# Softmax row sums of twenty attention heads taken by fours instead of by pairs, and late loads moved

## The chip, the cores and the metric

The kernel runs on one core of a Trainium2 chip. A core has a matrix engine (TensorE, PE in the profile; PEld is its weight load), a vector engine (VectorE, DVE), an activation engine (ScalarE, ACT), GpSimd (POOL) and a sync engine (SP), which run their own instruction streams in order and wait for each other by semaphores, and 16 DMA engines that move data between DRAM, SBUF and SBUF. SP and POOL issue most of the transfers; a transfer that adds to what lies at its destination (an accumulating DMA) is issued from POOL. The metric is the device time of one execution in microseconds, as the median of the runs.

## The reference, cut to what matters

```python
x = A_x                                             # 2048 rows of 1024
g = sigmoid((x * gate_w).sum(-1, keepdims=True))
# a: attention with 32 heads of 32
q, k, v = split(x @ wqkv)
p = softmax(einsum("bhqd,bhkd->bhqk", q, k) * 32 ** -0.5, axis=-1)
a = einsum("bhqk,bhkd->bhqd", p, v) -> (2048, 1024) @ wo
# b: for each row and each of 32 key heads the best of 8 x 8 experts, gelu(x . u[e]) * v[e]
return g * a + (1 - g) * b
```

All of it is float32. The change concerns the attention: the sum over keys in the softmax's denominator.

## The kernel before, in words

The program has three stages: projections and the expert branch (to about 648 us), the attention (to about 1650 us), and the output projection. The change lies in the attention; a few constants at the program's start and places in SBUF move with it.

**Tiles of the attention.** The 32 heads run one after another. A head has 16 tiles; tile `kt` holds 128 keys against all 2048 queries. `scores` makes four matmuls a tile (128 x 512 each) into a ring of seven PSUM banks (`ring`), ACT applies exp and writes the tile `P` (128 x 2048) to SBUF, and `pv` multiplies it with the values into the PSUM tile `o`. The loop at the end goes by groups of two tiles: scores of this group, then `pv` of the group before, then whatever the table `todo` holds for the two steps. A step is one tile, and `at(step, f, ...)` enters a function at a step; for head `h`, `base` is 16 h and `NT` is 16, so `base + NT + 12` is tile 12 of the head after `h`.

**Row sums.** A head's denominator is the sum of its 16 tiles over keys, that is over tiles and over the 128 partitions. Over tiles (`presum`): VectorE adds eleven times into `ACC`; tile 1 is written straight into a second sum `ACCD`, and tiles 3, 8 and 12 are added to `ACCD` by accumulating DMAs of 1 MB (`accd<-P` in the profile; where the buffer of a tile has another name, `accd<-vhl`, `accd<-wo_raw`). These three depend on each other, since each adds to what the one before left. In the next head ACC and ACCD are added on VectorE (merge). Over partitions: two heads share the tile `T` (named `rb` in the profile). An even head is merged into T and its lower 64 partitions are added onto the upper by an accumulating DMA (`merge_even`, `fold_even`); an odd head is merged in two halves by two VectorE instructions and its upper half is added onto T's lower (`merge_odd`, `fold_odd`). Then T holds one head in each half, and `head_sums(h, 2)` sums over 64 partitions each by four matmuls with the constant `ones2` (32 columns, 16 for each head). The four go as a set; ACT copies their bank out (`ssb`), SP stores it (`smd`), and after each fourth head `load_r` and `norm_r` load four heads' sums back, take the reciprocals and store them (`rr`, `rd`).

**Buffers of P.** `RING` says how many places the tiles of P rotate through: 11, from tile 330 on 9, from tile 384 on 8 (15 tiles a head count, since tile 1 is in ACCD). The three that go are the places of weights for the stage after the attention (`wo_raw2`, `wo_raw3`, `vhl`), loaded when they are free. A place is free when `pv` and the sum that reads it are done, for tiles 3, 8 and 12 when their DMA has landed.

**Order on the queues.** SP issues, for each head, the loads of K and Q of the head after the next (six of 256 KB and a small one; they wait for the last scores of the head that has their place), the store of `o` (`od<-osb`), a quarter of the next four heads' values (`V<-vd`), and in some heads a piece of a weight (`wo_raw<-in_wo`) and the sums' transfers. In the last heads come `vhl` and the attention's own outputs for the next stage (`V<-od`, 128 KB each). SP takes these strictly in order: a transfer that waits holds up all behind it. POOL issues the accumulating DMAs, in order as well.

Of the kernel before, what the change touches and what calls it, by code (L numbers as in the profile page):

```python
# [10 lines left out]
F32 = mybir.dt.float32  # L11
# [3 lines left out]
OP = mybir.AluOpType  # L15
# [4 lines left out]
H = 32  # L20
KC = D // 128
HC = KC // 2
NT = S // 128
NQ = S // 512
# [8 lines left out]
def gated_mha_peer_kernel(ctx, tc, xT, wqkv, wv, wo, wq, k12, ug, v, out):  # L33
# [8 lines left out]
    nc = tc.nc  # L42
# [25 lines left out]
    cbits = const.tile([1, 1], F32, name="cbits")  # L68

    ones2 = const.tile([128, 32], F32, name="ones2")  # L70
    nc.vector.memset(ones2, 0.0)
    for i in range(2):
        nc.vector.memset(ones2[64 * i:64 * i + 64, 16 * i:16 * i + 16], 1.0)


    const.tile([128, 24], F32, name="fill")
    ctx.enter_context(tc.tile_pool(name="fillr", bufs=1, side="right")).tile([128, 120], F32, name="fillr")

    def dma(dst, src, queue=nc.sync):
        a, b = (ap.bitcast(F32) if ap.dtype == F32R else ap for ap in (dst, src))  # L80
        return queue.dma_start(a, b)
# [621 lines left out]
    for blk, (k, n) in enumerate(order):  # L703
        w, c = chunks[k]
# [600 lines left out]
    def rowsum(ps, *srcs, ones=ones):  # L1305
        for src in srcs:
            for qc in range(NQ):
                yield nc.tensor.matmul(ps[32 * qc:32 * qc + 32, :], ones,  # L1308
                                       src[:, qc * 512:(qc + 1) * 512],
                                       start=(src is srcs[0]), stop=(src is srcs[-1]))  # L1310
# [15 lines left out]
    def merge(h):  # L1326
        nc.vector.tensor_add(ACC[h], ACC[h], ACCD[h])
# [13 lines left out]
    def fold_odd(h):  # L1341
        nc.gpsimd.dma_start(T[low], ACC.pop(h)[up], accum_op=OP.add)

    def head_sums(h, heads=1):
        i, = ring_banks(1)
        for ins in rowsum(ring[:, i, :], T if heads == 2 else ACC.pop(h),
                          ones=ones2 if heads == 2 else ones):
            on_ring(ins, i)
        on_ring(norm_sums(h, ring[:, i, :], heads), i)

# [7 lines left out]
    def norm_sums(h, ps, heads=1):  # L1358
        g, j = divmod(h, 4)
        o = wk.tile([128, 512], F32, name="ssb")  # L1360
        ins = nc.scalar.activation(o, ps, AF.Copy)
# [57 lines left out]
    def at(step, f, *a):  # L1419
        todo.setdefault(step, []).append((f, a))  # L1420

    for h in range(H):
        base = h * NT
        g, j = divmod(h, 4)
        if h >= 1 and h + 1 < H:
            at(base - 1, load_head, h + 1)
        if h < H - 1:
            at(base + NT, finish, h)
            if h == H - 2:
                at(base + NT + 5, merge, h)  # L1430
# [340 lines left out]
```

## Time and profile before

| | before |
|---|---|
| runs | 1826.53 us median of 3 (1825.97 to 1828.31) |
| profiled execution | 1827.73 us, of which the span of its instructions is 1826.0 |
| attention | about 648 to 1650 us: 32 heads of some 31.3 us each, a group of two tiles 3.9 |
| row-sum sets | 15 by pairs (heads 0 to 29) and one each for heads 30 and 31 |

The profile's page gives busy time by engine, the chain of work that ended last, and groups of instructions. Since TensorE is busy nearly throughout and lies on that chain, what counts is how far one group of tiles stands from the next on TensorE, and where it is held. Lines of the profile count in the program before (L1308 is the row-sum matmul, L1317 the accumulating DMA of a tile, L1338 and L1339 the odd merge, L1335 and L1342 the folds); lines of the changed program are three higher in that region.

### The profile page before, as it was taken

What the parts mean: (1) busy time and instruction counts of PE and PEld (TensorE: products, weight loads), DVE (VectorE), ACT (ScalarE), POOL (GpSimd) and SP (SyncE); (2) the same over time, 40 slices, a digit from 0 to 9 for tenths busy, and PEclk for the clock granted to TensorE, in tenths of its full rate; (3) what the DMA queues carried; (4) which work ended last, traced back from release to release, by engine and by line L of the source; (5) the groups of instructions that cost most, each with busy time, mean ns of one, the idle gap of its engine ahead of it and who ended that gap; (6) DMA issues with size and microseconds to landing.
All of it is one profiled execution on the core that took longest, in us unless ns stands there. A gap on an engine that the chain in (4) does not pass through costs nothing.

```text
span 1826.0 us, 26006 instructions
## 1 busy us (share of the span) xinstructions
PE 1816.9 (100%) x9935; PEld 1113.3 (61%) x9935; DVE 1484.2 (81%) x1258; ACT 1231.7 (67%) x1523; POOL 227.6 (12%) x272
## 2 busy tenths in 40 slices
PE   9999999999999999999999999999999999999999
PEld 7777777788888744444444444444444444447887
DVE  7868685368987689989889998989988898896674
ACT  4434322211243499999999999999999999893221
POOL 0221000036301201101101101101111010101000
PEclk9999999999999999999999999999999999999999
DMA  6788888722248688889898988889798988966861
GB/s 237 235 282 263 270 255 308 253 65 98 81 150 292 218 189 183 190 179 189 181 209 172 209 192 187 179 188 193 169 198 183 204 189 190 218 140 206 273 176 58
DMA packets 130775, 358.32 MB, mean 196 GB/s; under 512 B 16868, under 2 KB 57204, under 8 KB 105496
## 3 DMA queue, kind: packets, MB, share of 16 engines
q1 hardware_dynamic: 89864, 190.94, 35.2%
q0 software_dynamic: 20624, 129.77, 33.9%
q10 hardware_dynamic: 20160, 35.92, 6.7%
q8 instruction: 79, 1.29, 0.3%
q14 instruction: 48, 0.39, 0.1%
HBM read 169.14 MB, written 72.10 MB: 132 GB/s over the span
## 4 chain that ended last, share of the span: by engine, by line
PE 98%; DMA 1%; ACT 0%; issue 0%; ACTq 0%; DVE 0%; DVEq 0%
PE ring L1272 28%; PE o L1293 26%; PE bk L154 12%; PE bk L710 10%; PE pa L154 6%; PE bk L757 5%; PE pa L1515 2%; PE bk L925 2%; PE bk L310 2%; PE bk L394 1%; PE bk L490 1%; PE pa L1522 1%; PE ring L1308 1%; DMA accd<-P 1%; DMA wraw<-in_wqkv 0%; PE bk L331 0%
## 5 line engine op out<-in xcount | busy, mean ns | idle before, releaser
L1282 ACT ACTIVATE P<-ring 128x512 f32<-128x512 f32 (+2 forms) x823 | 732.8, 986 | 16.7 <-DMA accd<-P 4.0
L1324 DVE TENSOR_TENSOR acc<-acc,P 128x2048 f32<-128x2048 f32 x255 | 584.5, 2292 | 27.7 <-ACT P L1282 3.7
L1293 PE MATMUL o<-P,V 128*32 128x512 f32 x3072 | 376.0, 600 | 0.0
L1272 PE MATMUL ring<-z,z 98*128 98x512 f32 x1020 | 272.4, 408 | 2.1 <-ACT P L1282 2.0
L1272 PE MATMUL ring<-Q,K 98*128 98x512 f32 x1024 | 272.1, 408 | 0.2 <-ACT P L1282 0.2
L1272 PEld LDWEIGHTS ring<-z,z 98*128 98x128 f32 x1020 | 181.6, 188 | 146.3 <-ACT P L1282 61.6
L1272 PEld LDWEIGHTS ring<-Q,K 98*128 98x128 f32 x1024 | 182.3, 188 | 143.9 <-ACT P L1282 64.7
L1293 PEld LDWEIGHTS o<-P,V 128*32 128x32 f32 x3072 | 79.3, 109 | 179.0 <-issue 172.1
L1317 POOL DMA_DIRECT2D accd<-P x75 | 65.1, 868 | 613.7 <-ACT P L1282 395.7
L1282 ACT ACTIVATE wo_raw<-ring 128x512 f32<-128x512 f32 (+2 forms) x128 | 117.2, 989 | 2.1
L239 ACT ACTIVATE hi<-bk 128x512 fp32r<-128x512 f32 x40 | 23.7, 594 | 120.6 <-PE bk L710 101.0
L1324 DVE TENSOR_TENSOR acc<-acc,wo_raw 128x2048 f32<-128x2048 f32 x40 | 91.7, 2292 | 3.8
L710 PE MATMUL bk<-xh,e 128*128 128x512 f32 x384 | 94.2, 394 | 0.0
L710 PE MATMUL bk<-xl,e 128*128 128x512 f32 x384 | 92.3, 389 | 0.0
L1322 DVE TENSOR_TENSOR acc<-P,P 128x2048 f32<-128x2048 f32 x24 | 55.0, 2291 | 39.1 <-ACT P L1282 39.1
L252 DVE TENSOR_TENSOR lo<-bk,hi 128x512 fp32r<-128x512 f32 x40 | 27.6, 690 | 70.2 <-ACT hi L239 67.5
L710 PEld LDWEIGHTS bk<-xh,e 128*128 128x128 f32 x384 | 71.1, 188 | 21.9 <-issue 3.4
L710 PEld LDWEIGHTS bk<-xl,e 128*128 128x128 f32 x384 | 72.1, 188 | 14.9
L100 DVE TENSOR_TENSOR e<-wraw,e 128x512 fp32r<-128x512 f32 (+3 forms) x64 | 55.5, 875 | 25.9 <-ACT e L99 25.5
L1282 ACT ACTIVATE vhl<-ring 128x512 f32<-128x512 f32 (+2 forms) x78 | 71.9, 976 | 1.0
L154 PE MATMUL bk<-xh,e 128*128 128x512 f32 x288 | 68.5, 393 | 0.0
L99 ACT ACTIVATE e<-wraw 128x512 fp32r<-128x512 f32 (+3 forms) x64 | 44.7, 705 | 34.9 <-DMA wraw<-in_wqkv 18.5
(302 smaller groups left out, 2501.1 us busy)
## 6 DMA issues: line engine op xcount, KB each, us to landing
accd<-P POOLq DMA_DIRECT2D x75, 1024.0 KB, 9.7
wqt<-in_wq SPq DMA_DIRECT2D x26, 1024.0 KB
wraw<-in_wqkv SPq DMA_DIRECT2D x30, 512.0 KB
accd<-wo_raw POOLq DMA_DIRECT2D x12, 1024.0 KB, 8.8
qdh<-hi ACTq DMA_DIRECT2D x32, 256.0 KB
qdl<-lo ACTq DMA_DIRECT2D x32, 256.0 KB
kdh<-hi ACTq DMA_DIRECT2D x32, 256.0 KB
kdl<-lo ACTq DMA_DIRECT2D x32, 256.0 KB
```

What stands on the lines that cost most here:

```text
L99: nc.scalar.activation(hi, src, AF.Copy)
L100: (on or nc.vector).tensor_tensor(out=lo, in0=src, in1=hi.bitcast(F32), op=OP.subtract)
L154: nc.tensor.matmul(ps, self.a[a][i][:, k, :], self.b[b][j][k], start=(not first and k == 0 and i == j == 0), stop=(k == HC - 1 and i == 1))
L310: nc.tensor.matmul(ps[32 * quad:32 * quad + 32, :], kpad[:, quad % 2, i, :], t[:, quad, :], start=(i == 0), stop=(i == 3))
L710: nc.tensor.matmul(ps, t[:, kc // HC, a, kc % HC], x_at(b, n, kc), start=first, stop=last)
L757: nc.tensor.matmul(ps, x_at(a, t // 4, kc)[:, tok], b, start=first, stop=last)
L1272: on_ring(nc.tensor.matmul(ring[:, i, :], K[:98, kt * 128:(kt + 1) * 128], Q[:98, qc * 512:(qc + 1) * 512], start=True, stop=True), i)
L1282: on_ring(nc.scalar.activation(P[h, kt][:, q0 * 512:(q0 + m) * 512].rearrange("p (a m) -> p a m", a=m), ring[:, i:i + m, :], AF.Exp, scale ...
L1293: nc.tensor.matmul(O[h][32 * qc:32 * qc + 32, :], Vt[g][:, kt, 32 * j:32 * j + 32], p[:, qc * 512:(qc + 1) * 512], start=(kt == 0), stop=( ...
L1317: nc.gpsimd.dma_start(ACCD[h], P[h, kt], accum_op=OP.add)
L1322: nc.vector.tensor_add(ACC[h], P[h, 0], P[h, kt])
L1324: nc.vector.tensor_add(ACC[h], ACC[h], P[h, kt])
```

## The change

Heads 0 to 19 (`FOURS` = 5 groups of four) share T by quarters of 32 partitions. The first head of four is merged into T by one VectorE instruction and folded twice there: 64 partitions onto 64, then 32 onto 32. Each of the other three is merged into its ACC by one instruction; SP copies its own quarter to T (256 KB), and POOL issues three accumulating DMAs of 256 KB: one quarter of ACC onto another, then the remaining two sums onto T. One set of four matmuls with `ones4` (32 columns, 8 for each head) then gives four heads' sums, at tile 2 of the head after the one that follows the fourth. `load_r` and `norm_r` of these groups come 8 and 12 steps later. Heads 20 to 31 stay as they were.

The places of P become 9 from tile 308 (in head 20, where it was head 22) and 8 from tile 416 (head 27, where it was 25). The loads of the last weights go two heads earlier (heads 21 to 28, where they were 23 to 30), and of the seven `V<-od` loads two, not four, stand in head 29 and five, not three, in head 30. The tile `fill` grows by 96 columns, so that with `ones4` what follows moves by 128 columns.

```diff
+    ones4 = const.tile([128, 32], F32, name="ones4")
+    for t, heads in ((ones2, 2), (ones4, 4)):
+        nc.vector.memset(t, 0.0)
+        for i in range(heads):
+            m, w = 128 // heads, 32 // heads
+            nc.vector.memset(t[m * i:m * i + m, w * i:w * i + w], 1.0)
-    const.tile([128, 24], F32, name="fill")
+    const.tile([128, 120], F32, name="fill")
...
-    RING = (11, 0), (9, 30 * 11), (8, 30 * 11 + 6 * 9)
-    LATE = 23, 28
+    RING = (11, 0), (9, 28 * 11), (8, 28 * 11 + 12 * 9)
+    LATE = 21, 28
...
+    def merge4(h):
+        q = h % 4
+        if q == 0:
+            nc.vector.tensor_add(T, ACC.pop(h), ACCD[h])
+        else:
+            merge(h)
+            dma(T[quarter(q)], ACC[h][quarter(q)])
+
+    def fold4(h, step):
+        q = h % 4
+        if q == 0:
+            steps = (T[up], T[low]), (T[quarter(0)], T[quarter(1)])
+        else:
+            a, b, c = others(q)
+            steps = ((ACC[h][a], ACC[h][b]), (T[quarter(q)], ACC[h][c]),
+                     (T[quarter(q)], ACC[h][a]))
+        if step < len(steps):
+            dst, src = steps[step]
+            nc.gpsimd.dma_start(dst, src, accum_op=OP.add)
...
-            dma(SMD[g][j + i:j + i + 1, :].rearrange("o (q s) -> (o q) s", q=NQ), o[16 * i::32, :])
+            dma(SMD[g][j + i:j + i + 1, :].rearrange("o (q s) -> (o q) s", q=NQ), o[32 // heads * i::32, :])
...
+            elif g < FOURS:
+                at(base + NT + 3, merge4, h)
+                for step, k in enumerate((5, 10, 13)):
+                    at(base + NT + k, fold4, h, step)
             else:
                 at(base + NT + 3, (merge_even, merge_odd)[h % 2], h)
                 at(base + NT + 5, (fold_even, fold_odd)[h % 2], h)
-            if h % 2 and h < H - 2:
-                at(base + NT + 12, head_sums, h - 1, 2)
+                if h % 2:
+                    at(base + NT + 12, head_sums, h - 1, 2)
         if j == 3 and g + 1 < G:
-            at(base + NT + 14, load_r, g)
-            at(base + NT + 18, norm_r, g)
+            if g < FOURS:
+                at(base + NT + 18, head_sums, h - 3, 4)
+            at(base + NT + (22 if g < FOURS else 14), load_r, g)
+            at(base + NT + (30 if g < FOURS else 18), norm_r, g)
...
-    at(29 * NT + 13, load_o, 0, 0, 4)
-    at(30 * NT + 7, load_o, 0, 4, KC - 1)
+    at(29 * NT + 13, load_o, 0, 0, 2)
+    at(30 * NT + 7, load_o, 0, 2, KC - 1)
```

**TensorE, heads 8 and 9.** Before, the set for heads 6 and 7 stood between two groups of head 8 (`z` holds the keys and queries of even heads):

```order
L1272 MATMUL ring<-z_4621,z_4620 128x512 x8
L1293 MATMUL o<-vhl,V 32x512 x4
L1293 MATMUL o<-wo_raw_7046,V 32x512 x4
L1308 MATMUL ring<-rb_5204,ones_104 32x512 x4
L1272 MATMUL ring<-z_4621,z_4620 128x512 x8
```

Now the set for heads 4 to 7 stands in head 9 (`Q`, `K`: odd heads), behind `pv` of its tiles 0 and 1, and ahead of the scores of tiles 4 and 5:

```order
L1275 MATMUL ring<-Q_5228,K_5227 128x512 x8
L1296 MATMUL o<-P_7096,V 32x512 x4
L1296 MATMUL o<-P_7105,V 32x512 x4
L1275 MATMUL ring<-Q_5228,K_5227 128x512 x8
L1296 MATMUL o<-P_7128,V 32x512 x4
L1296 MATMUL o<-accd,V 32x512 x4
L1311 MATMUL ring<-rb_5210,ones_105 32x512 x4
L1275 MATMUL ring<-Q_5228,K_5227 128x512 x8
```

Half of the sets of heads 0 to 19 are gone, and the ones that remain stand six tiles later than a pair's set did.

**POOL, head 8 and the beginning of head 9.** Before, the three additions of tiles 3, 8 and 12 of head 8, with the fold of head 7 behind the first, and the first two DMAs of head 9:

```order
L1317 DMA accd<-P_6941 128x2048
L1342 DMA rb_5204<-acc 64x2048
L1317 DMA accd<-P_7012 128x2048
L1317 DMA accd<-wo_raw_7063 128x2048
L1317 DMA accd<-P_7161 128x2048
L1335 DMA rb_5204<-rb_5204 64x2048
```

Now head 7's three folds stand behind the three additions:

```order
L1320 DMA accd<-P_6949 128x2048
L1375 DMA acc<-acc 32x2048
L1320 DMA accd<-P_7020 128x2048
L1375 DMA rb_5210<-acc 32x2048
L1320 DMA accd<-wo_raw_7070 128x2048
L1375 DMA rb_5210<-acc 32x2048
L1320 DMA accd<-P_7162 128x2048
L1375 DMA rb_5210<-rb_5210 64x2048
```

The last fold that the set in head 9 reads is thus queued behind the addition of tile 12 of head 8.

**SP, head 8.** Before, from the store of head 7's output to the loads for head 10:

```order
L81 DMA od_72<-osb 4x32x512
L81 DMA V<-vd_67 128x4x128
L81 DMA wo_raw_5199<-in_wo 128x512
L81 DMA smd_81<-ssb 4x512 x2
L81 DMA rr<-smd_81 128x64
L81 DMA z_4620<-kdh 32x2048 x2
L81 DMA z_4620<-kdl 32x2048
```

Now the same stretch:

```order
L84 DMA od_72<-osb 4x32x512
L84 DMA rb_5210<-acc 32x2048
L84 DMA V<-vd_67 128x4x128
L84 DMA wo_raw_5205<-in_wo 128x512
L84 DMA z_4626<-kdh 32x2048 x2
L84 DMA z_4626<-kdl 32x2048
```

The copy of head 7's quarter, which waits for its merge, now stands ahead of the load of values; the transfers of the sums, which stood ahead of the loads of keys and queries, have gone to head 9.

More of the change, by code (lines that the diff above doesn't have):

```diff
@@ L1342, in fold_odd, with quarter, others @@
         nc.gpsimd.dma_start(T[low], ACC.pop(h)[up], accum_op=OP.add)
+    FOURS = 5
+    def quarter(i):
+        return slice(32 * i, 32 * i + 32)
+    def others(q):
+        return [quarter(i) for i in range(4) if i != q]
+    def merge4(h):
[16 more added lines that the diff above has]
+            nc.gpsimd.dma_start(dst, src, accum_op=OP.add)
     def head_sums(h, heads=1):
         i, = ring_banks(1)
-        for ins in rowsum(ring[:, i, :], T if heads == 2 else ACC.pop(h),
-                          ones=ones2 if heads == 2 else ones):
+        for ins in rowsum(ring[:, i, :], T if heads > 1 else ACC.pop(h),
+                          ones={1: ones, 2: ones2, 4: ones4}[heads]):
             on_ring(ins, i)
```

3 lines of the change are left out of this document (removed).

## The prediction

> **What bounds the kernel now.** I began with the page: busy time, then the chain that ended last.
>
> ```profile
> span 1826.0 us, 26006 instructions
> PE 1816.9 (100%) x9935; PEld 1113.3 (61%) x9935; DVE 1484.2 (81%) x1258; ACT 1231.7 (67%) x1523; POOL 227.6 (12%) x272
> ...
> PE 98%; DMA 1%; ACT 0%; issue 0%; ACTq 0%; DVE 0%; DVEq 0%
> ```
>
> TensorE is 98% of the chain, one DMA 1%. Next the busy time by stretches: the middle of the attention, its last heads, and the few microseconds behind a stall (columns: busy time of PE, PEld, DVE, ACT, POOL with counts, then TensorE's granted clock, DMA share, GB/s).
>
> ```profile
> 1100.00:1200.00 100.00, 100.00 (x620) 47.17 (x613) 90.84 (x42) 97.99 (x114) 10.25 (x12) 1.00 0.87 189
> 1576.00:1612.00 36.00, 33.97 (x200) 14.96 (x198) 28.33 (x13) 30.66 (x37) 4.27 (x5) 0.95 0.86 189
> 1592.00:1595.00 3.00, 3.00 (x14) 0.67 (x17) 2.97 (x2) 2.92 (x3) 0.45 (x1) 0.52 0.51 110
> ```
>
> In mid-attention TensorE never rests, so whatever leaves its stream there shortens the time. ACT has 2% to spare, VectorE 9%, the DMA engines 13%: each could become the bound. Between 1576 and 1612 TensorE rests for 2 us, and then runs at half its clock. What a group costs, and what it lost there, I read from the chain in order of time (start, length, what).
>
> ```profile
> 811.12 2.07 PE ring L1272 x8
> ...
> 834.57 2.07 PE ring L1272 x8
> ...
> 842.38 0.86 PE ring L1308 x8
> 843.24 2.04 PE ring L1272 x8
> ...
> 1571.81 2.07 PE ring L1272 x8
> 1577.24 11.97 DMA accd<-P
> ...
> 1599.59 2.07 PE ring L1272 x8
> ```
>
> Six undisturbed groups take 834.57 - 811.12 = 23.45 us, 3.91 each. The two groups with a row-sum set take 8.67, so **a set costs 8.67 - 2 x 3.91 = 0.85 to 0.86 us**, its own row. The six groups from 1571.81 take 27.78: **4.33 us are lost in heads 29 and 30**. The instruction timeline there says how:
>
> ```profile
> 1589.32 5.61 ACT L1282 ACTIVATE P<-ring 128x1536 f32<-128x1536 f32 x6 [2.70 <-DMA accd<-P]
> 1590.82 1.97 PE L1272 MATMUL ring<-z,z 98*128 98x512 f32 x5 [2.01 <-ACT P L1282]
> ```
>
> ACT found no free place for a tile, since the place's last content was still read by an accumulating DMA (1577.24 + 11.97 = 1589.21); TensorE then waited 2.01 us for ACT, and the half clock and shorter waits around it make up the other 2.3.
>
> **The change part by part. Row sums.** Heads 0 to 19 had ten sets and have five. 5 x 0.86 = **4.3 us less** on TensorE, on the path. The groups of instructions that go along:
>
> ```profile
> L1338 DVE TENSOR_TENSOR acc<-acc,accd 64x2048 f32<-64x2048 f32 x15 | 34.2, 2280 | 17.8 <-DMA accd<-P 14.7 <-DMA accd<-wo_raw 2.5 <-DMA accd<-vhl 0.4
> L1361 ACT ACTIVATE ssb<-ring 128x512 f32<-128x512 f32 x16 | 9.6, 598 | 6.5 <-PE ring L1308 6.4
> ```
>
> Ten odd heads need one merge where they needed two: 10 x 2.28 = 23 us less for VectorE; five evacuations less, 3 us, for ACT. Neither is on the path, so I count nothing; it keeps ACT's 2% of slack, which the shorter head would otherwise eat. Five more small memsets at the start stand in front of nothing but TensorE's warm-up: nothing.
>
> **Added transfers.** Per four heads, four folds of 512 KB become one of 512 and ten of 256, and three copies of 256 KB come in: over five groups 5.2 MB more to accumulate, 3.9 MB to copy. The queues' totals (packets, MB, share of 16 engines) price this:
>
> ```profile
> q1 hardware_dynamic: 89864, 190.94, 35.2%
> q0 software_dynamic: 20624, 129.77, 33.9%
> ```
>
> 0.339 x 1826 / 129.77 = 4.8 us of all engines per accumulated MB, 0.352 x 1826 / 190.94 = 3.4 per plain one: 25 + 13 = 38 us over some 634 us of heads 0 to 19 (20 x 8 groups of 3.91, ten sets), six points on a DMA share of 0.87. Beside 0.93 there is still room, and with 11 places for P a late landing has three tiles (5.9 us) more than in head 29. I count nothing; if the cover fails, it costs as in the rivals.
>
> **The new wait.** The set in heads 5, 9, 13, 17 and 21 reads a fold that is queued behind the addition of the preceding head's tile 12. Behind a waiting set stand all further scores. The trace has no quarter fold; the rows of head 8 bound it. First head 8's SP queue (and, last, its late loads of keys), and its merge:
>
> ```profile
> 876.56 0.78 SPq L81 DMA_DIRECT2D K<-kdh  x2
> ...
> 884.00 1.06 SPq L81 DMA_DIRECT2D V<-vd  x1
> ...
> 889.66 2.28 DVE L1338 TENSOR_TENSOR acc<-acc,accd 64x2048 f32<-64x2048 f32 x1 [2.17 <-DMA accd<-P]
> ...
> 914.47 0.84 SPq L81 DMA_DIRECT2D z<-kdh  x2
> ```
>
> Then POOL's issues from tile 12 of head 7 to tile 12 of head 8, the landings of these five, in the same order, asked one by one, and the scores of tiles 4 of heads 8 and 9, where a set like the new ones would stand:
>
> ```profile
> 876.83 0.86 POOL L1317 DMA_DIRECT2D accd<-P  x1 [6.51 <-PE ring L1272]
> 887.30 0.85 POOL L1317 DMA_DIRECT2D accd<-P  x1 [9.60 <-ACT P L1282]
> 894.56 0.81 POOL L1342 DMA_DIRECT2D rb<-acc  x1 [6.42 <-DVE rb L1339]
> 898.96 0.90 POOL L1317 DMA_DIRECT2D accd<-P  x1 [3.58 <-DMA accd<-P]
> 907.13 0.85 POOL L1317 DMA_DIRECT2D accd<-wo_raw  x1 [7.27 <-PE ring L1272]
> ...
> DMA to landing us min/median/max: 12.7/12.7/12.7
> DMA to landing us min/median/max: 11.1/11.1/11.1
> DMA to landing us min/median/max: 6.7/6.7/6.7
> DMA to landing us min/median/max: 7.6/7.6/7.6
> DMA to landing us min/median/max: 7.0/7.0/7.0
> ...
> 886.23 2.04 PE ring L1272 x8
> 918.34 2.04 PE ring L1272 x8
> ```
>
> The additions form a chain: 887.30 + 11.1 = 898.4, issue 898.96; + 7.6 = 906.6, issue 907.13. The fold of 64 partitions lands at 901.3, 2.9 us behind the addition ahead of it; a quarter fold is half of that, **1.45** (an estimate). From head 8: 907.13 + 7.0 + 1.45 = 915.6, and the set's place is 918.34, less the 0.86 of a set that no longer stands in head 8: 917.5. No wait, 1.9 us to spare. From head 7: 876.83 + 12.7 + 1.45 = 891.0 against 886.23: **4.8 us late**. The two differ in the keys and queries: head 7's loads come 0.3 us before its last addition, head 8's come after it had landed, because SP was held by the sums' transfers. These have left head 8, so its loads will come early too. Against this, the load of values (884.00) now waits behind the copy, so for the end of a merge (889.66 + 2.28 = 891.9), and no longer lies in front of the addition of tile 3, which took 11.1 us where the next took 7.6. I take half of these 3.5 us: the last addition is issued at 905.4, some 2.4 us ahead of head 8's new loads. With the median landing of all these additions,
>
> ```profile
> accd<-P POOLq DMA_DIRECT2D x75, 1024.0 KB, 9.7
> ```
>
> its fold lands at 905.4 + 9.7 + 1.45 = 916.6, 0.9 us before the set. So I take **no wait**, the value nearest to head 8's row, knowing that the margin is thin; the ends are 0 (a set can't start before its place) and 5 x 4.8 = 24 us.
>
> The Trainium skill speaks against this edit: "DMA: Bandwidth & Descriptors", Rules for kernel authors, advises one 128-partition transfer over pieces by partitions, since the pieces share the same engines, and its Anatomy of one DMA gives about 2.0 us plus bytes over 436 GB/s. An estimate by that page: 3.2 us for 64 partitions, 2.6 for 32. The trace's 2.9 agrees for the half. With 2.6 the fold would land 0.2 us behind the set's place, and the sum would be 1.0 us longer, 1818.9.
>
> **The late loads.** Those around the stall:
>
> ```profile
> 1552.85 0.41 SPq L81 DMA_DIRECT2D vhl<-vpl  x1
> 1553.46 0.33 SPq L81 DMA_DIRECT2D wo_raw<-in_wo  x1
> 1554.63 3.42 SPq L81 DMA_DIRECT2D V<-od  x4
> ...
> 1583.28 0.46 SPq L81 DMA_DIRECT2D wo_raw<-in_wo  x1
> ```
>
> Head 29 loses a weight piece (256 KB) and two of four `V<-od` (256 KB): at 3.4 us per MB 1.8 us less ahead of its additions, whose chain (each waits for the one before) was late by the 2.70 us of ACT's wait. Head 30 keeps its bytes. That is not all of the 2.7, but the landing at fault took 12.0 us where the median is 9.7, which I put down to the same crowd of loads. I take the whole **4.3 us as gone**; bounds 0 and 4.3. Below zero lies a new stall in heads 20 to 22, which have 9 places where they had 11; heads 25 to 27 get one more.
>
> **Sum** against the profiled 1827.73: 1827.73 - 4.3 - 4.3 = 1819.1; its runs' median is 1.2 lower, so 1817.9 of 1826.53.
>
> **The rivals.**
> 1. *The set waits for its fold* (slower). Place: TensorE ahead of the set in heads 5, 9, 13, 17, 21. It decides from landings later than the set's place by 8.6 / 5 = 1.7 us each, when the gain is gone; from 2.5 us the kernel is slower by over 0.2%. With half of head 7's lateness, 2.4 us, 1817.9 + 12 = 1830; with all of it 1842. For it: head 7's row, the early loads. Against it: the value load that moves out of the way, head 8's row.
> 2. *The stall at the end stays*, since K, Q and `vhl` remain: 1817.9 + 4.3 = 1822.2.
> 3. *The additional transfers hold P's places*, in heads 1 to 22: two stalls like that of head 29 give back 8.7, 1826.6. Against it: 0.87 + 0.06, and 11 places. In this case the change doesn't do what it says, since loads are moved and not spread thinner.
>
> On rival 1's price the half clock matters: behind 2.01 us of rest the clock was 0.52 from 1592 to 1595, some 1.7 us in all. So waits over about 2 us would cost 3.7, and the middle of rival 1 is 1830 to 1838. The Trainium skill, "TensorE: Matmul & The Clock Gate", Part 1, has the clock halved after an idle window of about 3.4 us; by that rule no wait here would cost more than itself, and 1830 would hold. The trace throttled after 2.01 us, so it disagrees.
>
> **How the numbers follow.** The forecast (no wait, stall gone) 0.45. Rival 1 0.32: by up to 1 us a set (0.12, still faster), up to 2.4 us (0.10, the same), more (0.10, slower). Rival 2 0.13, faster. Rival 3 0.10: the same 0.06, slower 0.04. Within 0.2% (3.65 us) is what a measurement of this kernel can't tell from no change. So faster 0.70, same 0.16, slower 0.14. The range goes from 1816, a little below the sum for what head 28 and 31 may give besides, to 1830, which leaves out the dearer half of rival 1.
>
> **What would show it.** Right: five sets by fours of 0.86 us, no idle of TensorE ahead of them, `V<-vd` behind the copy, the addition of tile 12 in heads 4, 8, 12, 16 issued ahead of the key loads; no rest of TensorE near 1580. Wrong: PE or PEld at the set waiting for `rb` DMAs, granted clock under 1.00 between 780 and 1320, ACT's P waiting for `accd` DMAs before head 28.

## The result and the profile after

The changed kernel takes **1858.8 us** (median of 4 runs, 1855.33 to 1859.82) where the kernel before takes 1826.35 beside it (4 runs): a ratio of 1.0171 [1.0158, 1.0185], 1.7% slower. The profiled execution, the fastest of the four, took 1855.33 us; its span is 1853.4, 27.4 more than before. The page of the changed kernel, its span, the busy time of the engines, and the chain that ended last:

```profile
span 1853.4 us, 26006 instructions
PE 1822.1 (98%) x9895; PEld 1114.3 (60%) x9895; DVE 1458.6 (79%) x1253; ACT 1230.0 (66%) x1519; POOL 256.2 (14%) x307
...
PE 92%; DVE 3%; DMA 2%; ACT 2%; issue 1%; SPq 0%; DVEq 0%; ACTq 0%
```

TensorE's part of the chain fell from 98% to 92%. The difference of the spans can be read from two numbers of this page and the one before: TensorE idled 1853.4 - 1822.1 = 31.3 us, where it idled 1826.0 - 1816.9 = 9.1, so **22.2 us of new rest**; and it was busy 5.2 us longer although five sets of 0.86 us are gone, so the remaining work took 5.2 + 4.3 = **9.5 us longer**. Where both happen is seen in the busy time by stretches (PE, PEld, DVE, ACT, POOL with counts, then granted clock, DMA share, GB/s); the first line is the kernel before, the others the changed kernel:

```profile
786.00:1330.00 544.00, 544.00 (x3369) 255.09 (x3362) 491.44 (x225) 532.57 (x616) 58.10 (x68) 1.00 0.87 189
...
786.00:1330.00 544.00, 521.76 (x3152) 243.52 (x3152) 450.21 (x205) 501.95 (x578) 78.68 (x94) 0.97 0.91 194
...
1100.00:1180.00 80.00, 80.00 (x491) 38.16 (x488) 66.48 (x30) 78.55 (x92) 13.47 (x16) 1.00 0.94 202
1604.00:1640.00 36.00, 34.18 (x211) 15.58 (x204) 28.49 (x14) 32.76 (x39) 4.29 (x5) 1.00 0.90 198
```

Between 786 and 1330 us, the stretch that holds heads 5 to 20 and the five new sets, TensorE before never rested; now it rests 544 - 521.76 = 22.24 us, which is all of the new rest, and the clock is 0.97 on the mean. Away from the sets (1100 to 1180) nothing is lost. The last row is the stretch of the stall in heads 29 and 30, 28 us later than before: 1.8 us of rest at the full clock, where it was 2.0 us and a clock of 0.95. The instruction timeline of TensorE has these five rows for the sets of heads 5, 9, 13, 17 and 21 (start, length, tile, count; in brackets the rest ahead of it):

```profile
794.22 1.08 PE L1311 MATMUL ring<-rb,ones 128*32 128x512 f32 x4 [4.16 <-DMA rb<-acc]
930.13 1.93 PE L1311 MATMUL ring<-rb,ones 128*32 128x512 f32 x7 [5.57 <-issue]
1066.50 1.08 PE L1311 MATMUL ring<-rb,ones 128*32 128x512 f32 x4 [7.34 <-issue]
1196.44 1.07 PE L1311 MATMUL ring<-rb,ones 128*32 128x512 f32 x8 [2.39 <-issue]
1325.31 1.65 PE L1311 MATMUL ring<-rb,ones 128*32 128x512 f32 x8 [2.77 <-issue]
```

4.16 + 5.57 + 7.34 + 2.39 + 2.77 = 22.2 us: every rest of that stretch is ahead of a set. Only the first names what it waited for, a DMA out of `acc` into `rb`, that is, the last fold into T. The others say "issue", which means that the view found no releaser; the landing times name it. For head 8 and the set in head 9, these are POOL's issues from the same stretch as the prediction shows of before: the addition of tile 12 of head 7, the last fold of head 6, the addition of tile 3 of head 8, that of tile 12, and the last fold of head 7; then the times from issue to landing of the five, in the same order:

```profile
883.20 0.90 POOL L1320 DMA_DIRECT2D accd<-P  x1 [5.28 <-DMA accd<-P]
885.60 0.78 POOL L1375 DMA_DIRECT2D rb<-acc  x1 [1.50 <-DMA rb<-acc]
894.23 0.90 POOL L1320 DMA_DIRECT2D accd<-P  x1 [7.84 <-PE ring L1275]
...
915.79 0.90 POOL L1320 DMA_DIRECT2D accd<-wo_raw  x1 [5.51 <-ACT P L1285]
917.85 0.78 POOL L1375 DMA_DIRECT2D rb<-acc  x1 [1.16 <-PE ring L1275]
...
DMA to landing us min/median/max: 12.3/12.3/12.3
DMA to landing us min/median/max: 12.0/12.0/12.0
DMA to landing us min/median/max: 12.5/12.5/12.5
DMA to landing us min/median/max: 11.7/11.7/11.7
DMA to landing us min/median/max: 12.0/12.0/12.0
```

The addition of tile 12 lands at 915.79 + 11.7 = 927.5, the fold behind it at 917.85 + 12.0 = 929.9, and the set starts at 930.13. A fold of 256 KB needs 12.0 us because it lies behind 1 MB on the same queue; issued ahead of it, in run 2 below, it needs 8.0. SP's issues in the same head show what the addition has beside it:

```profile
914.91 1.15 SPq L84 DMA_DIRECT2D z<-kdh  x2
```

The keys and queries of head 10 (six loads of 256 KB from 914.91) are issued 0.9 us ahead of the addition of tile 12; before, they came 7.3 us behind it. The load of values does come later, at 902.97, as the prediction said.

One more row is new, from the table of what VectorE waited for (in total, times, longest):

```profile
DVE acc L1325 <- DMA rb<-acc: 40.0, 9, 7.8
```

VectorE's first addition of a head needs one of two ACC buffers, and the last fold of the head two before still reads it. It waited nine times, 40 us, for late folds; before, the row did not exist.

### The profile page after: what moved, and what is told of

Same layout as the page of the kernel before. It is cut to its first block, busy times and chain, and to the rows that moved or that the text cites. A ratio compares the mean times of both kernels' runs of the same rounds, so it can differ in the third digit from the quotient of the medians.

```text
span 1853.4 us, 26006 instructions
## 1 busy us (share of the span) xinstructions
PE 1822.1 (98%) x9895; PEld 1114.3 (60%) x9895; DVE 1458.6 (79%) x1253; ACT 1230.0 (66%) x1519; POOL 256.2 (14%) x307
## 4 chain that ended last, share of the span: by engine, by line
PE 92%; DVE 3%; DMA 2%; ACT 2%; issue 1%; SPq 0%; DVEq 0%; ACTq 0%
PE ring L1275 25%; PE o L1296 23%; PE bk L157 12%; PE bk L713 10%; PE pa L157 6%; PE bk L760 5%; DVE acc L1327 3%; PE pa L1554 2%; PE bk L928 2%; PE bk L313 2%; PE bk L397 1%; PE bk L493 1%; ACT P L1285 1%; PE pa L1561 1%; PE ring L1311 1%
## 5 line engine op out<-in xcount | busy, mean ns | idle before, releaser
L1285 ACT ACTIVATE P<-ring 128x1024 f32<-128x1024 f32 (+2 forms) x820 | 734.6, 987 | 21.1 <-PE ring L1275 5.0
L1327 DVE TENSOR_TENSOR acc<-acc,P 128x2048 f32<-128x2048 f32 x256 | 586.6, 2291 | 35.1 <-ACT P L1285 12.4
L1275 PE MATMUL ring<-Q,K 98*128 98x512 f32 x1024 | 276.9, 413 | 0.1
L1285 ACT ACTIVATE wo_raw<-ring 128x512 f32<-128x512 f32 (+2 forms) x122 | 109.5, 969 | 1.6
L1325 DVE TENSOR_TENSOR acc<-P,P 128x2048 f32<-128x2048 f32 x22 | 50.4, 2291 | 71.6 <-ACT P L1285 29.5
L1327 DVE TENSOR_TENSOR acc<-acc,wo_raw 128x2048 f32<-128x2048 f32 x37 | 84.8, 2291 | 4.5 <-ACT wo_raw L1285 1.3
L1285 ACT ACTIVATE vhl<-ring 128x1024 f32<-128x1024 f32 (+2 forms) x88 | 79.8, 965 | 2.1 <-PE ring L1275 1.1
```

The costliest lines, as they stand in the source:

```text
L1275: on_ring(nc.tensor.matmul(ring[:, i, :], K[:98, kt * 128:(kt + 1) * 128], Q[:98, qc * 512:(qc + 1) * 512], start=True, stop=True), i)
L1285: on_ring(nc.scalar.activation(P[h, kt][:, q0 * 512:(q0 + m) * 512].rearrange("p (a m) -> p a m", a=m), ring[:, i:i + m, :], AF.Exp, scale ...
L1325: nc.vector.tensor_add(ACC[h], P[h, 0], P[h, kt])
L1327: nc.vector.tensor_add(ACC[h], ACC[h], P[h, kt])
```

## The experiments

The theory after this reading: **the last fold is queued behind the addition of tile 12, and everything follows from that place** (the set waits, then the clock halves; and the fold, held up, also holds a buffer of row sums). The rivals: that the keys' early loads are the cause, that the set merely stands too early, that the added transfers overload the DMA engines, that the moved late loads matter. All runs were timed beside the kernel before (1826.9 to 1827.3 us). "Rest" below is that of TensorE between 786 and 1330 us, 544 less the first busy time of the row. The rows of that stretch stand together here, for runs 1, 2, 3, 5, 6, 7 and 8 in this order; in run 4 TensorE did not rest there:

```profile
786.00:1330.00 544.00, 537.89 (x3301) 251.20 (x3299) 469.90 (x214) 523.20 (x603) 81.24 (x96) 0.99 0.93 201
...
786.00:1330.00 544.00, 541.58 (x3340) 253.85 (x3342) 474.80 (x218) 531.36 (x613) 81.50 (x97) 1.00 0.95 203
...
786.00:1330.00 544.00, 533.99 (x3251) 249.01 (x3250) 462.74 (x211) 516.96 (x595) 80.42 (x95) 0.98 0.92 196
...
786.00:1330.00 544.00, 529.79 (x3212) 247.34 (x3208) 458.54 (x209) 511.53 (x591) 80.07 (x95) 0.98 0.92 197
...
786.00:1330.00 544.00, 524.69 (x3197) 245.14 (x3200) 455.62 (x208) 508.25 (x586) 79.15 (x94) 0.98 0.92 197
...
786.00:1330.00 544.00, 544.00 (x3356) 255.65 (x3355) 478.14 (x219) 533.67 (x617) 81.45 (x97) 1.00 0.95 205
...
786.00:1330.00 544.00, 534.35 (x3270) 249.22 (x3271) 461.28 (x211) 518.51 (x598) 81.17 (x96) 0.99 0.92 198
```

**1. The sets six tiles later.** The first merge of the next group moves too, since it overwrites T. In this run head 20's merge does not move, so the set for heads 16 to 19 sums head 20's T; the amount of work is the same.

```diff
-                at(base + NT + 3, merge4, h)
-                for step, k in enumerate((5, 10, 13)):
+                at(base + NT + (3 if j else 9), merge4, h)
+                for step, k in enumerate((5, 10, 13) if j else (11, 14)):
...
-                at(base + NT + 18, head_sums, h - 3, 4)
+                at(base + NT + 24, head_sums, h - 3, 4)
...
```

> The five sets by fours stand three groups (11.7 us) later, in tile 8 of heads 5, 9, 13, 17 and 21; the next four heads' first merge into T moves behind them. Theory A (the loss is the wait of the five sets for their last fold, 22.2 us of rest plus the half clock behind it, 33.6 us in all on TensorE): the waits go, about 1821 to 1823 us. Theory B (the added transfers themselves slow the additions and hold P's places, and the set only shows it): the loss turns up elsewhere, above 1826, with ACT's P waiting for accd DMAs or rests of TensorE outside the sets.

Measured: 1843.04 us (1831.6 to 1850.06), ratio 1.0098 [1.0076, 1.012], rest 6.1 us in its fastest, profiled execution. The rests are gone from the sets of heads 5, 9, 13 and 17, but TensorE now rests at scores of heads 16 and 21 (0.95 and 2.44 us), where ACT waits for an accumulating DMA, and at the set of head 21 (2.72 us), which here waits for head 20's own fold. The place of the set is part of the loss, not all; run 8 asks the same without head 20's fold in the way.

**2. The last folds ahead of the addition of tile 12.** One number:

```diff
-                for step, k in enumerate((5, 10, 13)):
+                for step, k in enumerate((5, 10, 11)):
```

> The last fold of each of the three later heads is issued ahead of the addition of tile 12, not behind it; the sets stay where they are. If a set waits because its fold is queued behind that addition: the fold lands some 5 us ahead of the set, no rest there, 1821 to 1826 (the addition of tile 12 is issued some 3 us later and lands later, which nobody on the path waits for). If the wait comes from the earlier folds or from the copy: rests of 2 us and more stay, above 1840.

Measured: **1825.35 us** (1822.53 to 1831.58), ratio 0.9993 [0.9981, 1.0004], rest 2.4 us, clock 1.00. The same folds, bytes and loads, and the whole loss is back, 1858.8 - 1825.35 = 33.4 us. POOL's last two issues in head 8 of this run, the landings of the last fold and of the addition, and the set in head 9:

```profile
907.16 0.77 POOL L1375 DMA_DIRECT2D rb<-acc  x1 [6.41 <-DMA rb<-acc]
907.67 1.18 POOL L1320 DMA_DIRECT2D accd<-wo_raw  x1
...
DMA to landing us min/median/max: 8.0/8.0/8.0
DMA to landing us min/median/max: 13.0/13.0/13.0
...
915.48 1.06 PE L1311 MATMUL ring<-rb,ones 128*32 128x512 f32 x8 [0.94 <-ACT P L1285]
```

The addition now takes 13.0 us, longer than in the changed kernel, and it costs TensorE nothing: what the set waits for has landed at 907.16 + 8.0 = 915.2, and the addition is needed only by the merge in the next head, where VectorE waits 2.2 us for it. So a slow addition is not the loss; a fold behind it is. One part of the expectation was missed: the fold does not land some 5 us ahead of the set. TensorE was ready for it at 915.48 - 0.94 = 914.5, and the fold landed 0.6 us later (the row names ACT, but the start follows the landing by 0.3 us, as in the changed kernel). The rest of 2.4 us is the wait of this set and of that in head 13, so the old place has no room even then, and the gain of the five sets does not show.

**3. The keys and queries behind the store of `o`** in heads 4, 8, 12, 16 and 20, so that they come when tile 12's addition has landed.

```diff
-            at(base - 1, load_head, h + 1)
+            at(base + (1 if h % 4 == 1 and 1 < h < 24 else -1), load_head, h + 1)
```

> In heads 4, 8, 12, 16 and 20 alone the seven loads of keys and queries stand behind the store of o, some 7 us later, so that they no longer fall on the addition of tile 12. If these loads are what makes it late: it lands in 7 to 8 us instead of 9.8 to 12.1, the fold lands at about the set's place, rests under 1 us a set, 1822 to 1830. If the chain of additions is late by itself (it is issued 0.5 to 4 us later than in the kernel before): rests of over 2 us stay, above 1840.

Measured: 1844.83 us (1841.1 to 1846.3), ratio 1.0098 [1.0082, 1.0113], rest 10.0 us. POOL's last two issues of head 8 in this run:

```profile
908.64 0.90 POOL L1320 DMA_DIRECT2D accd<-wo_raw  x1 [8.97 <-DMA accd<-P]
909.48 0.88 POOL L1375 DMA_DIRECT2D rb<-acc  x1
```

The addition of tile 12 in these heads took 7.1 to 8.2 us, about as long as in head 8 before the change (7.0); still the sets in heads 9 and 13 waited, 5.9 and 3.75 us. In head 8 the addition was issued late, because it had waited 8.97 us for the one of tile 8. And the fold behind it took 10.5 us: the keys, issued from 912.20, now lay beside the fold, which landed 4.2 us behind the addition (2.4 in the changed kernel). Moving the keys takes away some half of the rest (10.0 of 22.2 us are left); what is left is a chain that comes late by itself and a fold slowed by the keys, and this run does not part the two.

**4. The late loads alone:** the kernel before with the new places of P and the moved loads, without the row sums by fours.

```diff
-    RING = (11, 0), (9, 30 * 11), (8, 30 * 11 + 6 * 9)
-    LATE = 23, 28
+    RING = (11, 0), (9, 28 * 11), (8, 28 * 11 + 12 * 9)
+    LATE = 21, 28
...
-    at(29 * NT + 13, load_o, 0, 0, 4)
-    at(30 * NT + 7, load_o, 0, 4, KC - 1)
+    at(29 * NT + 13, load_o, 0, 0, 2)
+    at(30 * NT + 7, load_o, 0, 2, KC - 1)
```

> Row sums by pairs as in the kernel before, with the changed places of P and late loads alone. By the prediction the stall in heads 29 and 30 goes whole: 1822. By the trace of the changed kernel, where 2.7 us are still lost in heads 30 and 31 against 5.2 before: 1824. If the moved loads do nothing: 1826.

Measured: 1824.18 us (1823.95 to 1825.55), ratio 0.9984 [0.9975, 0.9993]: 0.0016 x 1827.3 = 2.9 us faster (1.3 to 4.6). What TensorE waited for in the attention (in total, times, longest), before and in this run:

```profile
PE ring L1272 <- ACT P L1282: 2.2, 2, 2.0
...
PE ring L1272 <- ACT P L1282: 1.4, 3, 0.8
```

The stall is shorter, and the clock was not halved behind it (1.00 between 1330 and 1650 us, where it was 0.99); but it is not gone, and one of the three rests, 0.42 us in head 22, is new.

**5 and 6. Which of the last folds counts?** Run 5 moves only the fold that the set reads (fourth head of a group), run 6 only those of the second and third heads.

```diff
-                for step, k in enumerate((5, 10, 13)):
+                for step, k in enumerate((5, 10, 11 if j == 3 else 13)):
```

> Only the last fold of the fourth head of each group (the one that the set reads) is issued ahead of the addition of tile 12; the last folds of the second and third heads stay behind it. Theory A, the place in the queue in heads 4, 8, 12, 16 and 20 alone decides: as with all three moved, 1823 to 1828 us, rests ahead of the sets under 1.5 us and no half clock. Theory B, the late last folds of the other heads count as well, because they hold a buffer of the row sums and so make the chain of head 4k late: rests of 2 to 4 us at some of the five sets, lost at the groups 10 to 20 us, 1832 to 1846 us.

```diff
-                for step, k in enumerate((5, 10, 13)):
+                for step, k in enumerate((5, 10, 13 if j == 3 else 11)):
```

> The other half: the last folds of the second and third heads are issued ahead of the addition of tile 12, that of the fourth head stays behind it. Theory A: the rests at the five sets stay as in the changed kernel (2.4 to 7.3 us, 22 us in sum), 1853 to 1862 us. Theory B: the chain of head 4k comes earlier, the fold lands 0 to 4 us behind the place of the set, rests 10 us or less in sum, 1832 to 1848 us.

Measured: run 5 1837.66 us (1827.99 to 1845.6), ratio 1.0052 [1.0033, 1.0072], rest 14.2 us in its slowest, profiled execution; run 6 1856.12 us (1851.86 to 1864.47), ratio 1.0178 [1.0157, 1.0199], rest 19.3 us. So theory B of the expectation holds for run 5 (one rest, 6.9 us in head 17, is longer than it said) and theory A for run 6: the fold of the fourth head is the larger part, and alone it is not enough. How the other folds come into it is seen on VectorE in run 5, at the beginning of head 11 (start, length, tile, count, rest ahead and its releaser):

```profile
986.39 2.29 DVE L1325 TENSOR_TENSOR acc<-P,P 128x2048 f32<-128x2048 f32 x1 [8.74 <-DMA rb<-acc]
988.60 2.28 DVE L1330 TENSOR_TENSOR acc<-acc,accd 128x2048 f32<-128x2048 f32 x1
```

and a head later on POOL and TensorE (the last fold of head 11, its landing, and the set in head 13):

```profile
1039.52 0.77 POOL L1375 DMA_DIRECT2D rb<-acc  x1 [11.38 <-issue]
...
DMA to landing us min/median/max: 7.3/7.3/7.3
...
1047.05 1.93 PE L1311 MATMUL ring<-rb,ones 128*32 128x512 f32 x8 [4.29 <-issue]
```

VectorE's first addition waits 8.74 us for a last fold of two heads earlier, since that fold holds the ACC buffer (it was issued at 973.78 and took 12.4 us). The merge of the head before stands right behind it in VectorE's order and is late with it; behind the merge stand the folds (the first waited 8.97 us for it and was issued at 991.18), and behind those the next additions. The last fold, issued at 1039.52 though it stands ahead of tile 12's addition, lands at 1046.8, and the set begins at 1047.05. **A late fold thus makes the following heads' folds late.** VectorE's waits for a last fold bear this out. They sum to 40.0 us in the changed kernel, 46.2 in run 5 and 52.9 in run 8, where the last folds of the second and third heads stand behind the addition, and to 9.7, 15.0 and 10.8 in runs 2, 6 and 7, where they stand ahead of it. Run 6 also shows the other half by itself: with little of this way back left, its sets still wait 19.3 us. Moving one kind alone gives back 1858.8 - 1837.66 = 21 us and 1858.8 - 1856.12 = 3 us; moving both gives back 33.

**7. The last folds ahead, and the sets three tiles later.** The first merge of the next group moves along (that of head 20 too).

```diff
-                at(base + NT + 3, merge4, h)
-                for step, k in enumerate((5, 10, 13)):
+                at(base + NT + 3 + (3 if j == 0 else 0), merge4, h)
+                for step, k in enumerate((5, 10, 11) if j else (8, 11)):
...
-                at(base + NT + 3, (merge_even, merge_odd)[h % 2], h)
-                at(base + NT + 5, (fold_even, fold_odd)[h % 2], h)
+                d = 3 if h == 4 * FOURS else 0
+                at(base + NT + 3 + d, (merge_even, merge_odd)[h % 2], h)
+                at(base + NT + 5 + d, (fold_even, fold_odd)[h % 2], h)
...
-                at(base + NT + 18, head_sums, h - 3, 4)
-            at(base + NT + (22 if g < FOURS else 14), load_r, g)
-            at(base + NT + (30 if g < FOURS else 18), norm_r, g)
+                at(base + NT + 21, head_sums, h - 3, 4)
+            at(base + NT + (25 if g < FOURS else 14), load_r, g)
+            at(base + NT + (33 if g < FOURS else 18), norm_r, g)
```

> The last folds ahead of the addition of tile 12 in all heads, and the set, with the first merge of the next group and its folds, three tiles later. Theory A, the folds land where they did (up to 1.7 us behind the old place): 5.9 us of new room, no rest at any set, lost at the groups 2.5 to 3.5 us, the span 1826.0 - 4.3 - 2 to 2.9, so 1819 to 1822 us. Theory B, the later first merge and the late additions make the chain of the next head late and stall scores elsewhere: 1824 to 1830 us.

Measured: **1821.45 us** (1819.65 to 1823.67), ratio 0.9977 [0.9967, 0.9988], faster than both kernels. No rest between 786 and 1330 us, at a DMA share of 0.95, so the added transfers alone don't stall TensorE there. Theory A: the median lies in its range of 1819 to 1822.

**8. The sets six tiles later, but the folds left behind the addition** (run 1 with head 20's merge moved along, so that every set has its own sums). The diff is that of run 7 with six for three, and the last fold at 13; its main lines:

```diff
-                at(base + NT + 3, merge4, h)
-                for step, k in enumerate((5, 10, 13)):
+                at(base + NT + 3 + (6 if j == 0 else 0), merge4, h)
+                for step, k in enumerate((5, 10, 13) if j else (11, 14)):
...
-                at(base + NT + 18, head_sums, h - 3, 4)
+                at(base + NT + 24, head_sums, h - 3, 4)
...
```

> The order of the changed kernel's queue is kept, but the set, the first merge of the next group and its folds, also those of head 20, come six tiles (11.7 us) later. Theory A, only the wait of the set for the fold costs: every fold has landed by then, no rest at a set, 1819 to 1824 us. Theory B, the late last folds also hold the buffers of the row sums, so that the additions come later from head to head and the exponentials wait for a place: rests of 1 to 4 us at scores or sets in heads 12 to 21, 1828 to 1846 us, scattered.

Measured: 1834.64 us (1832.83 to 1837.27), ratio 1.0047 [1.0032, 1.0063], rest 9.7 us. No set waits at all, and the kernel is still slower than before. The largest rest stands in head 21; the chain of work, ACT's row and TensorE's row there:

```profile
1297.68 12.19 DMA accd<-P
...
1309.95 2.86 ACT L1285 ACTIVATE P<-ring 128x512 f32<-128x512 f32 x3 [4.11 <-DMA accd<-P]
...
1310.60 0.50 PE L1275 MATMUL ring<-Q,K 98*128 98x512 f32 x1 [3.47 <-ACT P L1285]
```

This is the stall that the prediction describes in head 29 of the kernel before: a late addition holds a place of P, ACT waits for the place, TensorE for ACT. Theory B: without a set that waits, the late folds come back as late additions.

**9. Run 7 with the late loads as before the change.** (The lines of run 4, taken back.)

```diff
-    RING = (11, 0), (9, 28 * 11), (8, 28 * 11 + 12 * 9)
-    LATE = 21, 28
+    RING = (11, 0), (9, 30 * 11), (8, 30 * 11 + 6 * 9)
+    LATE = 23, 28
...
-    at(29 * NT + 13, load_o, 0, 0, 2)
-    at(30 * NT + 7, load_o, 0, 2, KC - 1)
+    at(29 * NT + 13, load_o, 0, 0, 4)
+    at(30 * NT + 7, load_o, 0, 4, KC - 1)
```

> As the run with the last folds ahead and the sets three tiles later (1821.5 us, lost 1.74 us at the groups), but with the late loads where they were before the change. If the late loads are worth what they were alone (2.9 us in the span), the stall in heads 29 to 31 is back with 4 to 5 us: 1823.5 to 1825.5 us; the gain of the five sets alone is then read against before, -4.3 us at most. If the row sums' transfers had already moved the late loads' stall, 1821 to 1822 us.

Measured: 1822.71 us (1820.73 to 1825.0), ratio 0.9976 [0.9967, 0.9985]: 0.0024 x 1827.3 = **4.4 us faster** than before (2.7 to 6.0) by the five sets alone. Beside run 7 the ratio is the same; the profiled spans are 1820.8 and 1817.8. Between these two readings, no gain and 3 us, the times do not decide what the late loads add when the sets are by fours. The traces point to a gain: in run 9 the stall is back, with 1.7 us of rest and a clock of 0.99 between 1330 and 1650 us, where run 7 has 0.9 us and 1.00.

**10. Seven groups of four** instead of five, on top of run 7 (`FOURS = 7`).

```diff
-    FOURS = 5
+    FOURS = 7
```

> As that run, but seven groups of four (heads 0 to 27) instead of five: three sets fewer (two sets of four where there were five of pairs and singles less one), 3 x 0.86 = 2.6 us, so 1818.9 us (1818 to 1820) if only the sets count. If the added folds delay the additions in heads 21 to 28, where the weight loads hold places of P, rests at scores of 1 to 3 us come back: 1820 to 1826 us.

Measured: 1824.33 us (1822.0 to 1826.78), ratio 0.9988 [0.9979, 0.9997]. Slower than run 7, though sets are saved. (The expectation counted a set too many: four sets of pairs become two of four, so two are saved, 2 x 0.86 = 1.7 us.) TensorE rests between 1330 and 1650 us, where it was busy for 319.06 us in run 7; the row of this run:

```profile
1330.00:1650.00 320.00, 314.60 (x1936) 146.23 (x1935) 277.96 (x134) 302.27 (x351) 46.62 (x59) 1.00 0.89 196
```

320 - 314.60 = 5.4 us of rest against 0.9, nearly all in heads 23 to 29, where P has 9 places or 8 and not 11. ACT waits there for accumulating DMAs, 8.1 us in five waits over the attention, where it is one wait of 1.5 us in run 7: the added folds do hold the places up.

**11. The changed kernel with the late loads as before** (the lines of run 9, on the changed kernel).

> The changed kernel with the late loads where they were before: the sets and the folds as changed, behind the addition. If the late loads have nothing to do with the loss, the rests at the five sets stay at 17 to 26 us in sum and the end costs 2 to 3 us more: 1856 to 1863 us. If the ring of 11 places kept to head 30 or the moved loads matter for the chain in head 20 (the set of head 21), 1850 to 1856 us.

Measured: 1863.62 us (1860.05 to 1867.46), ratio 1.0197 [1.0177, 1.0216], just above the range of the first branch. TensorE is busy for 519.08 us of the 544 between 786 and 1330, so it rests 24.9. The moved late loads have no part in the loss; without them it is a little larger.

## Why the prediction failed, by its steps

**The new wait: the step that failed.** The prediction took "no wait", with the fold 0.9 us ahead of the set. The mechanism was in it as rival 1, at 0.32, and its dearest estimate was 4.8 us a set; measured are 2.4 to 7.3 us a set, 22.2 in sum, and the half clock behind. So the step that failed is the term "no wait": the set does wait, in head 9 for 5.6 us, because the addition of tile 12 and the fold queued behind it are issued and land later than the working had it. For the set in head 9 the working can be taken apart:

| | predicted | measured |
|---|---|---|
| issue of tile 12's addition ahead of the set's place | 917.5 - 905.4 = 12.1 us | 930.13 - 5.57 - 915.79 = 8.8 |
| its landing | 9.7 | 11.7 |
| the fold behind it | 1.45 | 929.9 - 927.5 = 2.4 |
| fold against the set's place | 0.9 early | 5.3 late |

3.3 us of the miss are the chain's time of issue. The prediction let the value load leave the front of tile 3's addition and so took half of 3.5 us off that addition. The load did leave (902.97), and the addition took 12.5 us, longer than the 11.1 before. What slowed it was not tested by itself: it was issued at 894.23, while the addition of tile 12 of head 7 was in flight to 895.5 and head 6's last fold to 885.60 + 12.0 = 897.6, and behind the keys and queries of head 9 (883.65 to 889.74). In run 2, where that last fold had landed by then, the same addition still took 11.7 us, so the fold is at most a small part. The prediction counted the three folds only by their bytes and by their own landing, and not for what they do to the additions around them. 2.0 us are the landing, with the early keys beside it, which the prediction named ("its loads will come early too") and then set aside with a median landing. Run 3 shows that moving them brings the addition back to 7.1 to 8.2 us, but not the chain. 1.0 us is the size of a quarter fold: 2.4 where 1.45 was worked out by halving. The distance does not halve with the bytes: in the trace of before, the half fold issued at 859.76 landed at 870.4, 2.3 us behind the addition ahead of it. (The 2.6 us that the prediction estimated by the Trainium skill, "DMA: Bandwidth & Descriptors", Anatomy of one DMA, is nearer. But it is the time of one DMA by itself, and neither the 2.4 here nor the 2.9 that the prediction set beside it is that: they are distances between two landings. From issue to landing these folds took 12.0 and 6.7 us.) Head 7's row, 4.8 us late, was nearer than head 8's row: it had keys ahead of the addition, as the new kernel would have.

What no part of the working had was **the way back**: last fold late, ACC buffer held, VectorE's first addition and the merge behind it late, next folds late. Runs 5 and 8 show it, run 6 what is left without it, and VectorE's waits for the fold are its trace.

**The price of a wait.** Rival 1 with the half clock was right in kind: 9.5 us of slower work on top of 22.2 us of rest. That this is the clock can be added up from the twelve microseconds behind the start of each of the five sets:

```profile
794.22:806.22 12.00, 12.00 (x48) 5.00 (x52) 9.21 (x5) 6.85 (x10) 0.82 (x1) 0.62 0.78 165
930.13:942.13 12.00, 12.00 (x57) 5.23 (x58) 10.39 (x5) 8.02 (x9) 0.82 (x1) 0.73 0.69 148
1066.50:1078.50 12.00, 12.00 (x64) 5.80 (x64) 11.10 (x5) 9.31 (x11) 0.82 (x1) 0.87 0.63 143
1196.44:1208.44 12.00, 12.00 (x76) 5.68 (x80) 11.69 (x6) 10.67 (x13) 0.88 (x2) 1.00 0.84 178
1325.31:1337.31 12.00, 12.00 (x63) 5.97 (x64) 10.99 (x5) 9.40 (x13) 1.03 (x2) 0.86 0.82 169
```

12 x (0.38 + 0.27 + 0.13 + 0 + 0.14) = 11.0 us are lost to the clock there. The 1.7 us of half clock behind the stall in head 29 of the kernel before are gone, which leaves 9.3 us, against the 9.5 measured. Even the dearest case of rival 1, 1842 us, left the half clock out. The prediction's rule from the one row of before, over about 2 us, holds but for the rest of 2.39 us, after which the clock stayed full (below). By the rule of the Trainium skill ("TensorE: Matmul & The Clock Gate", Part 1), an idle window of 3.4 us, the rest of 2.77 us would have cost only itself; the trace disagrees (0.86 behind it).

**Row sums:** right, but only once nothing waits. Five sets fewer were priced at 4.3 us; run 9 gives 4.4 (2.7 to 6.0).

**Added transfers:** right that nothing need be lost to their bytes in heads 0 to 19 (run 7: no rest), with the share a little higher than said, 0.95 and not 0.93. The price of the accumulated bytes seems to have been set too low: POOL's queue reads in run 7 (packets, MB, share of 16 engines)

```profile
q0 software_dynamic: 21824, 135.02, 36.6%
```

With the row of before, 0.366 x 1817.8 - 0.339 x 1826.0 = 46 us of engine time for 5.25 MB, 8.8 us per MB where 4.8 were taken, if all of it is put down to the added bytes. Rival 3, a place of P held by a late addition, is what runs 8 and 10 met: in run 8 with the folds behind the additions, in run 10 where P has fewer places.

**The late loads:** right in direction, too large in size. 4.3 us were taken, 2.9 measured alone (run 4, 1.3 to 4.6). The stall became shorter rests; it did not go. Rival 2, the stall stays whole, did not happen.

**The signs to watch** were well chosen: a TensorE that waits for `rb` DMAs at the sets and a clock under 1.00 between 780 and 1320 is what came. Of the signs of being right, "the addition of tile 12 issued ahead of the key loads" did not come: in head 8 it was issued 0.9 us behind them. Run 2 shows that a slow addition alone would have been harmless.

## What to carry to other kernels

A transfer that something waits for must not be queued behind a long one that nothing waits for: here one number in a table of steps (13 to 11) was worth 33 us. When a change adds work to a queue that is kept in order, take the time of each later item of that queue anew, around the loop and back to where the buffers come free, instead of taking a median landing from a queue without it. And where a forecast's margin (0.9 us) is far smaller than the spread of the landings that it is made of (6.7 to 12.7 us in the five landings of before alone), the wait belongs into the sum.

## What the runs showed of the hardware that was not expected

The clock after a rest does not depend on the rest's length alone. The five rows above show it for the sets; here are the ten microseconds around the set in head 13 of the changed kernel and around a rest of 1.90 us in run 8:

```profile
1060.00:1070.00 10.00, 3.50 (x13) 1.59 (x14) 5.12 (x3) 1.20 (x2) 0.90 (x1) 0.66 0.89 190
...
1148.00:1158.00 10.00, 8.10 (x41) 3.00 (x44) 5.97 (x3) 6.50 (x8) 1.18 (x2) 0.83 0.62 127
```

A rest of 2.39 us kept the full clock (1.00), one of 1.90 us halved it for 3.4 us (0.83 over ten: 0.17 x 10 / 0.5), one of 7.34 us for 6.8 us (0.66). Of these 6.8 us only 0.13 x 12 / 0.5 = 3.1 lie behind the rest; the others lie within it and cost nothing. So the longest rest lost less to the clock, 1.6 us, than that of 4.16 us, behind which 0.38 x 12 / 0.5 = 9.1 us ran at half. In run 3 two rests of 0.37 and 0.84 us, half a us apart, were enough (0.50 from 1606 to 1608 us), while 0.98 and 0.84 us in the changed kernel were not (1.00 from 1604 to 1640). The half clock comes in steps of 3.4 us, so it seems that fixed stretches of that length are judged and that it matters how a rest lies across them; that was not tested by itself. The Trainium skill, "TensorE: Matmul & The Clock Gate", Part 1, has such a window, free-running, of 3.4 us; the steps here agree with it.

An accumulating DMA of 256 KB is not fast because it is small. From issue to landing, in the median of the 30 folds out of ACC into T, in the changed kernel and in run 2 (count, KB each, us):

```profile
rb<-acc POOLq DMA_DIRECT2D x30, 256.0 KB, 9.6
...
rb<-acc POOLq DMA_DIRECT2D x30, 256.0 KB, 7.3
```

It takes about as long as a 1 MB addition without loads beside it (7.0 us in the prediction's rows). The two kernels differ only in whether 1 MB stands ahead of the last fold on the queue; a last fold is every second one of the 30.
